# A cached-attention decode step with a gated FFN on one core: the order of the key transposes, the place of the PV matmuls, a layout of the FFN rows and a slot for the down weights

## The chip, the cores and the metric

The kernel runs on one core of a Trainium2 chip. The metric is device time in microseconds (us), the median of several executions. Five engines run their own instruction streams and meet only in semaphores: PE (TensorE, matmul), DVE (VectorE), ACT (ScalarE), POOL (GpSimd) and SP (SyncE, which here only issues DMAs).

## The reference

Four tokens (one for each of four batches) pass through two branches, which a gate mixes.

```python
q = (x @ wq)                                   # 4 x 32 heads x 128
k, v = k_cache[:, :, -4096:, :], v_cache[...]  # 8 key heads per batch, each for 4 query heads
p = softmax(q k^T / sqrt(128));  a = (p v) @ wo
gate = x @ W_gate; up = x @ W_up               # 512 -> 1792
b = (relu(gate) * up) @ W_down                 # 1792 -> 512
out = g * a + (1 - g) * b,  g = sigmoid(sum(x * gate_w))
```

All inputs are bf16. Keys and values of the window are 4 x 8 x 4096 x 128 each, so that nearly all of the 81 MB that the kernel reads is cache.

## The kernel before, in words

The 32 pairs of batch and key head are worked off in eight **sets** of four heads (s = 0 to 7; `NSET`). One set's keys are 4 MiB, and so are its values. SP issues every load, in the order of `_dma_order`: k0, x, gate_w, wq, k1, v0, then k(s), v(s-1) for s = 2 to 7, then the gate and up weights (wg, wu), v7, the down weights (wd) and the output weights (wo, in six pieces, `WO_PIECES`). The large loads go in turn into four slots of SBUF (`_slots`); a load waits until the slot's former content has been used: keys until their fourth transpose, values until the set's PV matmuls are done, wq until Q, wg until the gate and up matmuls. SP is one queue, so a load that waits holds back all that follow. In the kernel before, wd has no slot: it goes into the tile `kt`, over the transposed keys, and so waits for the last score matmul of set 7; wo takes the next slot in turn, which k7 held.

The work of the engines is written as one list of items (`_order`, L139). PE runs the items in this order, and the lists of DVE and ACT are derived from it: an item of PE appends the items of the other engines that evacuate it. For one set the items are:

- `KT(s, f)`, f = 0 to 3 (DVE, `EKT`, L506): transposes block f of the keys from the slot into `kt[:, f]`. It waits for the load of the keys and for the last reader of that part of `kt`, `SC(s-1, f)`.
- `SC(s, f)` (PE): eight matmuls of 512 columns and one for a mask, into one of three PSUM banks. DVE evacuates it (`ESC`, L534) into `sc` and keeps the row maximum. `ESC(s, 0)` waits for `EXP(s-1)`, because there is one tile `sc`.
- after `SC(s, 3)`: `MAX` (DVE, L538 and L540), `SW` (one small matmul that spreads the maxima over the rows of a head), `ESW` (DVE, L545 and L546, which gives `negmax`) and `EXP` (ACT, L612, `pe` from `sc`).
- `PT(s)` (DVE, `EPT`, L550): transposes `pe` into `pT`. There is one tile `pe`, so that `EXP(s)` waits for `PT(s-1)`.
- `RS(s)`: a small matmul for the sums of the rows; DVE makes the reciprocal.
- `PV(s)` (PE): 32 matmuls of 512 columns on the values of set s. ACT scales the result (`NORM`, L590), `OQ(s)` (16 small matmuls) turns it, ACT copies it (`EOQ`, L597).

Set s is pipelined against set s-1 by the list: in the loop over s, the softmax and PV of set s-1 stand between the score blocks of set s. The list of the kernel before is, for s from 1:

```python
o += [("KT", s, 0), ("PT", s - 1), ("KT", s, 1), ("SC", s, 0), ("KT", s, 2), ("SC", s, 1), ("KT", s, 3), ("SC", s, 2)]
o += [("RS", s - 1), ("PV", s - 1), ("SC", s, 3), ("SW", s), ("OQ", s - 1)]
```

After set 7 follow `PT(7)`, `RS(7)`, `GU` (gate and up matmuls: for each 16 matmuls, four column groups of the array side by side, the four groups taking 448 neighbouring columns each), ReLU on ACT (L605) and the product on DVE (`H`, L558), `HT` (56 matmuls of 4 columns that turn the rows of h), `PV(7)`, `OQ(7)`, `FFN` (28 matmuls with wd), `T2` (DVE, L566) and `WO` (64 matmuls, piece by piece as wo lands). `FIN` (L570) mixes, and two stores end the program. All matmuls are issued by one helper, which is why they share L314.

Of the kernel before, what the change touches and what calls it, by code (L numbers as in the profile page):

```python
# [8 lines left out]
ALU = mybir.AluOpType  # L9
# [128 lines left out]

def _order():  # L139
    o = [("XT",), ("Z",), ("KT", 0, 0), ("KT", 0, 1), ("KT", 0, 2), ("KT", 0, 3), ("Q",), ("QT",)]  # L140
    o += [("SC", 0, f) for f in range(4)] + [("SW", 0)]
    for s in range(1, NSET):
        o += [("KT", s, 0), ("PT", s - 1), ("KT", s, 1), ("SC", s, 0), ("KT", s, 2), ("SC", s, 1), ("KT", s, 3), ("SC", s, 2)]
        o += [("RS", s - 1), ("PV", s - 1), ("SC", s, 3), ("SW", s), ("OQ", s - 1)]
    s = NSET - 1
    o += [("PT", s), ("RS", s), ("GU",), ("HT",), ("PV", s), ("OQ", s), ("FFN",)]
    return o + [("WO", p) for p in range(len(WO_PIECES))]


# [7 lines left out]
def _slots():  # L157

    frees = [[] for _ in range(NSLOT)]
    at, wait = {}, {}  # L160
    turn = 0
    for it in _dma_order():
        k = it[0]
        if k in ("x", "gw", "wd") or (k == "wo" and it[1] > 0):
            continue
        if k == "wu":
            at[it] = at[("wg",)]
            wait[it] = wait[("wg",)]
# [5 lines left out]
        frees[n] = {"k": [("E", "KT", it[-1], 3)], "v": [("PV", it[-1])], "wq": [("Q", 1)], "wg": [("GU", 1)], "wo": []}[k]  # L174
    return at, wait


def _program(nc, plan, R, aps):
# [16 lines left out]

    Wq = slot("wq").rearrange("p (t f) -> p t f", t=4)
    Wg, Wu = slot("wg")[:, 0:4 * FF], slot("wg")[:, 4 * FF:8 * FF]
    Wd = kt[:, :, :].rearrange("p f c -> p (f c)")[:, 0:14 * 512]
    Wo = slot("wo", 0).rearrange("p (i c) -> p i c", i=32)
    grelu, hrow = sc[:, 0:448], sc[:, 512:960]  # L200

    trf, scf = {}, {}
    for it in order:
# [39 lines left out]
    def sync(e):  # L243
# [5 lines left out]
        for it in _dma_order():  # L249
# [4 lines left out]
            elif k == "gw":  # L254
                load(("GW",), "d_gw", gwT[:, :], gate_w.rearrange("(p t) -> p t", t=4))
            elif k == "wq":
                load(("WQ",), "d_wq", slot("wq"), A_wq.rearrange("(p t) f -> p (t f)", t=4), waits=w)
            elif k == "wg":
                load(("WG",), "d_wg", Wg, B_W_gate.rearrange("(p t) f -> p (t f)", t=4), waits=w)
            elif k == "wu":  # L260
                load(("WU",), "d_wu", Wu, B_W_up.rearrange("(p t) f -> p (t f)", t=4), waits=w)
            elif k == "wd":
                load(("WD",), "d_wd", Wd, B_W_down.rearrange("(p i) c -> p (i c)", i=14),
                     waits=[("SC", NSET - 1, 3)])
            elif k == "wo":
# [44 lines left out]
    def tensor(t):  # L310
# [73 lines left out]
        def OQ(s):  # L384
            key = ("OQ", s)
            r = 64 * (s // 4)
            for t in range(2):
                for cc in range(2):
                    for c in range(4):
# [106 lines left out]
    def vector(v):  # L496
# [58 lines left out]
            E.op(lambda: v.reciprocal(recip[:, s % 2:s % 2 + 1], banks[tr(key)][:, 0:1]), ev=("E",) + key, waits=[key])  # L555

        def H():
            E.op(lambda: v.tensor_tensor(hrow, grelu, banks[scb(("GU", 1))][:, 0:448], ALU.mult), ev=("H",),  # L558
                 waits=[("RELU",), ("GU", 1)])
            plan.ev[("E", "GU", 1)] = plan.ev[("H",)]  # L560

        def EHT():
            E.op(lambda: v.tensor_copy(hT[:, :], banks[tr(("HT",))][:, 0:56]), ev=("E", "HT"), waits=[("HT",)])
# [13 lines left out]
    def scalar(a):  # L577
# [24 lines left out]
                     ev=("GE",) if u else None, waits=[("Z",)])  # L602

        def RELU():
            E.op(lambda: a.activation(grelu, banks[scb(("GU", 0))][:, 0:448], ACTF.Relu), ev=("RELU",),  # L605
                 waits=[("GU", 0), ("EXP", NSET - 1)])
            plan.ev[("E", "GU", 0)] = plan.ev[("RELU",)]

# [41 lines left out]
```

## Time and profile before

| what | value |
|---|---|
| median of 3 runs | 207.85 us (207.54 to 209.7) |
| the profiled execution: own time, span | 209.0 us, 207.3 us |
| busy, of the span | PE 136.1 us (66%), DVE 127.0 us (61%), ACT 31.3 us (15%) |
| DMA | 81.16 MB, 392 GB/s over the span, 92.3% of 16 engines' span |
| mean granted PE clock | 0.876 |

The span is the time from the first to the last instruction of the profiled execution, and its own time is what was measured around it. A busy share is an average over the whole span: it tells that no single compute engine is full, not what each stage waits for. For that one reads the chain of waits, which goes back from the last instruction to what released it each time, and windows, which give busy time, granted clock and DMA rate of one stretch. SP's rows tell when a load was issued; the DMA view gives the time from the issue to the landing. PE's clock is granted by a throttle: 1.00 is full and 0.50 half.

### The profile page before, as it was taken

Reading aid. Unit: us, or ns where it says so; the run is one execution under the profiler, and the core shown is the slowest. Engines: PE = TensorE matmul, PEld = TensorE weight load, DVE = VectorE, ACT = ScalarE, POOL = GpSimd, SP = SyncE. Lnnn points to the kernel's source line nnn. Section 1 sums busy time; section 2 is a strip of 40 time slices with the busy share of each in tenths; the row PEclk is TensorE's granted clock in tenths of the full one; section 3 lists DMA queues with packets and bytes.
Section 4 is the critical chain, followed back from the end, with each engine's and each line's share of the span. In section 5 each row is a group of like instructions: output and inputs, shape, how many; then the busy total and the mean of one; then the engine's idle time right before and its main releaser. Section 6 shows DMA issues by size and latency. Waiting matters only on the chain.

```text
span 207.3 us, 2287 instructions
## 1 busy us (share of the span) xinstructions
PE 136.1 (66%) x936; PEld 60.8 (29%) x936; DVE 127.0 (61%) x193; ACT 31.3 (15%) x72; POOL 14.0 (7%) x38
## 2 busy tenths in 40 slices
PE   0010363991798459758966793789399766956975
PEld 0000131330243214322522251243234322522543
DVE  6039382128982997299649936991998299525000
ACT  2000036004001400140022014001400140033010
POOL 7774000000000000000000000000000000000000
PEclk9999995599589988967996999699769969996699
DMA  5999999999977999999999999999999999849950
GB/s 202 462 418 430 413 411 462 436 408 444 443 335 304 405 506 402 335 436 417 405 411 477 424 411 432 455 424 408 468 424 424 396 443 443 373 123 417 422 215 1
DMA packets 3923, 81.16 MB, mean 392 GB/s; under 512 B 572, under 2 KB 584, under 8 KB 968
## 3 DMA queue, kind: packets, MB, share of 16 engines
q1 hardware_dynamic: 3904, 81.01, 92.3%
q8 instruction: 7, 0.11, 0.2%
q14 instruction: 4, 0.03, 0.0%
q10 hardware_dynamic: 8, 0.00, 0.0%
HBM read 81.01 MB, written 0.00 MB: 391 GB/s over the span
## 4 chain that ended last, share of the span: by engine, by line
PE 46%; DVE 37%; DMA 10%; issue 3%; ACT 2%; SPq 1%; DVEq 0%; ACTq 0%
PE bank L314 45%; DVE kt L506 20%; DMA slots<-in_A_wq_dram 10%; DVE pT L550 8%; DVE sc L534 4%; DVE qblk L493 2%; ACT pe L612 1%; PE bank L318 1%; ACT qblk L587 1%; DVE rd L540 1%; SPq L247 1%; DVE hmax L545 1%; DVE negmax L546 1%; DVE rowmax L538 1%; ACT osb L590 0%
## 5 line engine op out<-in xcount | busy, mean ns | idle before, releaser
L314 PE MATMUL bank<-kt,qblk 128*128 128x512 bf16 x256 | 75.8, 446 | 27.0 <-DVE kt L506 24.9
L506 DVE STREAM_TRANSPOSE kt<-slots 128x2048 f32<-128x2048 f32 x32 | 73.2, 2294 | 0.0
L534 DVE TENSOR_SCALAR_CACHE_REDUCE sc<-bank 128x512 bf16<-128x512 f32 x32 | 21.4, 668 | 41.6 <-PE bank L314 41.6
L314 PEld LDWEIGHTS bank<-kt,qblk 128*128 128x128 bf16 x256 | 25.4, 108 | 72.5 <-DVE kt L506 33.5
L314 PE MATMUL bank<-slots,pT 128*64 128x512 bf16 x256 | 30.4, 393 | 0.0
L612 ACT ACTIVATE pe<-sc,negmax 128x2048 bf16<-128x2048 bf16 x8 | 16.0, 2002 | 35.7 <-DVE negmax L546 35.7
L590 ACT ACTIVATE osb<-bank,recip 128x512 bf16<-128x512 f32 x8 | 5.5, 687 | 101.6 <-PE bank L314 101.6
L550 DVE STREAM_TRANSPOSE pT<-pe 128x2048 bf16<-128x2048 bf16 x8 | 18.5, 2312 | 2.2 <-ACT pe L612 2.2
L314 PEld LDWEIGHTS bank<-slots,pT 128*64 128x64 bf16 x256 | 14.3, 113 | 12.4 <-issue 1.5
L314 PE MATMUL bank<-maskr,maskl 128*128 128x512 bf16 x32 | 13.6, 424 | 0.0
L314 PE MATMUL bank<-slots,xT 128*4 128x512 bf16 (+1 forms) x64 | 6.4, 571 | 9.6 <-DMA slots<-in_A_wq_dram 9.6
L318 PE MATMUL bank<-identb,xsb 4*128 4x4 bf16 x4 | 0.3, 173 | 13.4 <-DMA xsb<-in_A_x_dram 13.4
L314 PE MATMUL bank<-rd,grpb 128*128 128x8 bf16 x8 | 1.3, 168 | 10.9 <-DVE rd L540 9.3
L314 PE MATMUL bank<-osb,fold 128*64 128x32 bf16 x128 | 5.4, 184 | 0.8 <-ACT osb L590 0.8
L314 PEld LDWEIGHTS bank<-slots,xT 128*4 128x4 bf16 x64 | 1.8, 111 | 12.5 <-DMA slots<-in_A_wq_dram 9.7
L566 DVE TENSOR_SCALAR t<-bank,gg 128x256 f32<-128x256 f32 x1 | 0.5, 484 | 7.8 <-PE bank L314 7.8
L510 DVE COPY xT<-bank 128x16 bf16<-128x16 bf16 x1 | 0.2, 167 | 8.2 <-PE bank L318 8.2
L314 PEld LDWEIGHTS bank<-osb,fold 128*64 128x64 bf16 x128 | 4.6, 112 | 1.5 <-ACT osb L590 1.3
L314 PEld LDWEIGHTS bank<-rd,grpb 128*128 128x128 bf16 x8 | 0.8, 95 | 14.7 <-issue 12.9
L314 PEld LDWEIGHTS bank<-maskr,maskl 128*128 128x128 bf16 x32 | 3.4, 106 | 5.3 <-issue 2.5
L493 DVE COPY qblk<-bank 32x32 bf16<-32x32 bf16 x32 | 4.0, 179 | 0.9 <-PE bank L318 0.8
L318 PEld LDWEIGHTS bank<-identb,xsb 4*128 4x128 bf16 x4 | 0.2, 115 | 13.4 <-DMA xsb<-in_A_x_dram 13.4
(56 smaller groups left out, 63.9 us busy)
## 6 DMA issues: line engine op xcount, KB each, us to landing
slots<-in_A_k_cache_dram SPq DMA_DIRECT2D x8, 4096.0 KB, 15.9
slots<-in_A_v_cache_dram SPq DMA_DIRECT2D x8, 4096.0 KB, 22.5
slots<-in_A_wq_dram SPq DMA_DIRECT2D x1, 4096.0 KB, 21.4
slots<-in_A_wo_dram SPq DMA_DIRECT2D x3, 1024.0 KB, 12.0
slots<-in_B_W_gate_dram SPq DMA_DIRECT2D x1, 1792.0 KB, 10.7
slots<-in_B_W_up_dram SPq DMA_DIRECT2D x1, 1792.0 KB, 14.6
kt<-in_B_W_down_dram SPq DMA_DIRECT2D x1, 1792.0 KB, 7.0
slots<-in_A_wo_dram SPq DMA_DIRECT2D x1, 512.0 KB, 14.6
```

The costliest lines, as they stand in the source:

```text
L247: E.op(lambda: e.dma_start(dst, src), ev=ev, waits=waits, ctr=ctr)
L314: E.op(lambda: t.matmul(out_, lhsT, rhs, start=start, stop=stop, tile_position=pos, skip_group_check=True), ev=ev, waits=waits)
L318: E.op(lambda: t.transpose(out_, in_, idn), ev=ev, waits=waits)
L493: E.op(lambda dst=dst, r=r, g=g, e=e, src=src: copy(dst, src[r, g, 0:B, e, :, :]), ev=("E",) + key if (q, g, e) == (3, 1, 1) else None, wa ...
L506: E.op(lambda: v.transpose(kt[:, f, :].bitcast(FP32), slot("k", s)[:, 4096 * f:4096 * f + 4096].bitcast(FP32)), ev=("E", "KT", s, f), waits=w)
L534: E.op(lambda: v.tensor_scalar(sc[:, 512 * f:512 * f + 512], banks[scb(key)], 1.0, None, op0=ALU.mult, op1=ALU.max, accum_out=mx4[:, f:f + ...
L538: E.op(lambda: v.tensor_reduce(rowmax[:, :], mx4[:, :], AXIS.X, ALU.max), ev=("RMX", s), waits=[("E", "SC", s, 3)])
L540: E.op(lambda: v.tensor_scalar(rd8[:, :], R["own8"][:, :], rowmax[:, 0:1], None, op0=ALU.mult), ev=("MAX", s), waits=[("RMX", s), ("OWN", ...
L545: E.op(lambda: v.tensor_reduce(hmax[:, :], banks[tr(key)][:, 0:8], AXIS.X, ALU.max), ev=("E",) + key, waits=[key])
L550: E.op(lambda: v.transpose(pT[:, s % 2, :], pe[:, :]), ev=("E", "PT", s), waits=[("EXP", s)] + ([("PV", s - 2)] if s >= 2 else []))
L590: E.op(lambda: a.activation(osb[:, s % 2, :], ob(s), ACTF.Copy, scale=recip[:, s % 2:s % 2 + 1]), ev=("NORM", s), waits=[("E", "RS", s), ( ...
L612: E.op(lambda: a.activation(pe[:, :], sc[:, :], ACTF.Exp, bias=negmax[:, s % 2:s % 2 + 1], scale=SCALE, accum_out=rowsum[:, s % 2:s % 2 + ...
```

## The change

Four things are changed.

1. **The order of the list.** `KT(s, 0)` stands ahead of `SC(s-1, 3)`, so that on DVE the first key transpose of the next set runs before the fourth score block of the set before it is evacuated. `PV(s-1)` stands behind `SC(s, 2)` as before, but `SC(s, 3)` is now in the next turn of the loop, behind `KT(s+1, 0)`. `OQ` stands ahead of `SW`, and `PT(s-1)` behind `KT(s, 1)`.
2. **A slot for wd.** wd takes the next slot in turn, the one of k7, and so waits for the fourth key transpose of set 7; wo moves to the slot that v6 held, and waits for `PV(6)`.
3. **GU by residues.** Column group j takes the 128 columns of each index i = j, j+4, ... instead of 448 neighbouring ones. The moving operand is read with a step of 14 elements (28 bytes), in 512 columns (j = 0, 1) or 384 (j = 2, 3) instead of 448.
4. **HT whole.** Four transposes of 128 x 128 in place of 56 small matmuls; `RELU` and `H` work on 512 columns instead of 448, and the copy `EHT` picks the 56 columns from the bank.

```diff
 def _order():
-    o += [("SC", 0, f) for f in range(4)] + [("SW", 0)]
+    o += [("SC", 0, 0), ("SC", 0, 1), ("SC", 0, 2)]
     for s in range(1, NSET):
-        o += [("KT", s, 0), ("PT", s - 1), ("KT", s, 1), ("SC", s, 0), ("KT", s, 2), ("SC", s, 1), ("KT", s, 3), ("SC", s, 2)]
-        o += [("RS", s - 1), ("PV", s - 1), ("SC", s, 3), ("SW", s), ("OQ", s - 1)]
+        o += [("KT", s, 0), ("SC", s - 1, 3)] + [("OQ", s - 2)] * (s > 1) + [("SW", s - 1), ("KT", s, 1), ("PT", s - 1)]
+        o += [("SC", s, 0), ("KT", s, 2), ("SC", s, 1), ("RS", s - 1), ("KT", s, 3), ("SC", s, 2), ("PV", s - 1)]
     s = NSET - 1
-    o += [("PT", s), ("RS", s), ("GU",), ("HT",), ("PV", s), ("OQ", s), ("FFN",)]
+    o += [("SC", s, 3), ("OQ", s - 1), ("SW", s), ("PT", s), ("RS", s), ("GU",), ("HT",), ("PV", s), ("OQ", s), ("FFN",)]
...
-        if k in ("x", "gw", "wd") or (k == "wo" and it[1] > 0):
+        if k in ("x", "gw") or (k == "wo" and it[1] > 0):
...
-    Wd = kt[:, :, :].rearrange("p f c -> p (f c)")[:, 0:14 * 512]
+    Wd = slot("wd")[:, 0:14 * 512]
...
-                     waits=[("SC", NSET - 1, 3)])
+                     waits=w)
...
+        def gu_n(j):
+            return 512 if j < 2 else 384
+
+        def gu_cols(W, q, j):
+            g = W[:, FF * q:FF * q + FF].rearrange("p (k i) -> p i k", i=14)
+            return g[:, j:14:4, :]
...
-                        mm(banks[scb(fill)][32 * j:32 * j + 4, 0:448], xT[:, 4 * q:4 * q + 4],
-                           W[:, FF * q + 448 * j:FF * q + 448 * j + 448], q == 0, q == 3,
+                        mm(banks[scb(fill)][32 * j:32 * j + 4, 0:gu_n(j)], xT[:, 4 * q:4 * q + 4],
+                           gu_cols(W, q, j), q == 0, q == 3,
...
-            for i in range(14):
-                for j in range(4):
-                    r = slice(32 * j, 32 * j + 4)
-                    mm(banks[tr(key)][32 * j:32 * j + 32, 4 * i:4 * i + 4], hrow[r, i:448:14], identb[r, r], True, True,
-                       ev=key if (i, j) == (13, 3) else None, waits=tr_free(key) + [("H",), ("IDB",)],
-                       pos=(32 * j, 32 * j))
+            for g in range(4):
+                tp(bankb[tr(key)][:, 128 * g:128 * g + 128], hrow[:, 128 * g:128 * g + 128], identb[:, :],
+                   ev=key if g == 3 else None, waits=tr_free(key) + [("H",), ("IDB",)])
```

How the list moves the instructions is shown at three places. The first is DVE in the middle of the program, one turn of the loop, from the evacuation of the fourth score block of a set on; `kt<-slots` is a key transpose, `pT<-pe` the transpose of the probabilities, `sc,mx4<-bank` the evacuation of a score block, `rowmax` to `negmax` the softmax's maxima. Before:

```order
L534 TENSOR_SCALAR sc,mx4<-bank4 128x512
L538 TENSOR_REDUCE rowmax<-mx4 128x1
L540 TENSOR_SCALAR rd8<-own8,rowmax 128x8
L545 TENSOR_REDUCE hmax<-bank1 128x1
L546 TENSOR_SCALAR negmax<-hmax 128x1
L506 STREAM_TRANSPOSE kt<-slots 128x2048
L550 STREAM_TRANSPOSE pT<-pe 128x2048
L506 STREAM_TRANSPOSE kt<-slots 128x2048
L534 TENSOR_SCALAR sc,mx4<-bank2 128x512
L506 STREAM_TRANSPOSE kt<-slots 128x2048
L534 TENSOR_SCALAR sc,mx4<-bank3 128x512
L506 STREAM_TRANSPOSE kt<-slots 128x2048
```

And the same turn in the changed kernel, whose lines are four further down for the same code:

```order
L510 STREAM_TRANSPOSE kt<-slots 128x2048
L538 TENSOR_SCALAR sc,mx4<-bank4 128x512
L542 TENSOR_REDUCE rowmax<-mx4 128x1
L544 TENSOR_SCALAR rd8<-own8,rowmax 128x8
L549 TENSOR_REDUCE hmax<-bank0 128x1
L550 TENSOR_SCALAR negmax<-hmax 128x1
L510 STREAM_TRANSPOSE kt<-slots 128x2048
L554 STREAM_TRANSPOSE pT<-pe 128x2048
L538 TENSOR_SCALAR sc,mx4<-bank2 128x512
L510 STREAM_TRANSPOSE kt<-slots 128x2048
L538 TENSOR_SCALAR sc,mx4<-bank3 128x512
```

Between `negmax` and the third key transpose of the set there stood two key transposes and `pT`; now one key transpose and `pT`, and the first key transpose stands ahead of the fourth evacuation.

The second place is PE over the same stretch; `slots,pT` is PV, `kt,qblk` with `maskr,maskl` a score block, `rd8,grpb` is SW, `osb,fold` OQ and `rowsum,grpf` RS. Before:

```order
L314 MATMUL bank6<-slots,pT 64x512 x32
L314 MATMUL bank3<-kt,qblk 128x512 x8
L314 MATMUL bank3<-maskr,maskl 128x512
L314 MATMUL bank0<-rd8,grpb 128x8
L314 MATMUL bank1<-osb,fold 64x32 x16
L314 MATMUL bank4<-kt,qblk 128x512 x8
```

In the changed kernel:

```order
L314 MATMUL bank5<-slots,pT 64x512 x32
L314 MATMUL bank4<-kt,qblk 128x512 x8
L314 MATMUL bank4<-maskr,maskl 128x512
L314 MATMUL bank1<-osb,fold 64x32 x16
L314 MATMUL bank0<-rd8,grpb 128x8
L314 MATMUL bank2<-kt,qblk 128x512 x8
```

On PE, OQ now stands ahead of SW (and RS, outside these rows, one score block earlier); the first score block of the next set follows as before, but the key transpose that it waits for now stands earlier on DVE.

The third place is the end of SP's queue, with the engine that each load waits for:

```order
 L247 DMA slots<-in_A_v_cache_dram 128x1x16384 [waits pe]
-L247 DMA kt<-in_B_W_down_dram 128x7168 [waits pe]
-L247 DMA slots<-in_A_wo_dram 128x4096 [waits dve]
+L247 DMA slots<-in_B_W_down_dram 128x7168 [waits dve]
+L247 DMA slots<-in_A_wo_dram 128x4096 [waits pe]
 L247 DMA slots<-in_A_wo_dram 128x4096 x2
```

The down weights wait for DVE (the last key transpose) instead of PE (the last score block), and the first piece of wo for PE (`PV(6)`).

More of the change, by code (lines that the diff above doesn't have):

```diff
@@ L173, in _slots @@
         wait[it] = list(frees[n])
-        frees[n] = {"k": [("E", "KT", it[-1], 3)], "v": [("PV", it[-1])], "wq": [("Q", 1)], "wg": [("GU", 1)], "wo": []}[k]
+        frees[n] = {"k": [("E", "KT", it[-1], 3)], "v": [("PV", it[-1])], "wq": [("Q", 1)], "wg": [("GU", 1)], "wd": [], "wo": []}[k]
     return at, wait
@@ L197, in _program @@
     Wg, Wu = slot("wg")[:, 0:4 * FF], slot("wg")[:, 4 * FF:8 * FF]
-    Wd = kt[:, :, :].rearrange("p f c -> p (f c)")[:, 0:14 * 512]
+    Wd = slot("wd")[:, 0:14 * 512]
     Wo = slot("wo", 0).rearrange("p (i c) -> p i c", i=32)
-    grelu, hrow = sc[:, 0:448], sc[:, 512:960]
+    grelu, hrow = sc[:, 0:512], sc[:, 512:1024]
     trf, scf = {}, {}
@@ L557, in H @@
         def H():
-            E.op(lambda: v.tensor_tensor(hrow, grelu, banks[scb(("GU", 1))][:, 0:448], ALU.mult), ev=("H",),
+            E.op(lambda: v.tensor_tensor(hrow, grelu, banks[scb(("GU", 1))], ALU.mult), ev=("H",),
                  waits=[("RELU",), ("GU", 1)])
@@ L562, in EHT @@
         def EHT():
-            E.op(lambda: v.tensor_copy(hT[:, :], banks[tr(("HT",))][:, 0:56]), ev=("E", "HT"), waits=[("HT",)])
+            ht_src = bankb[tr(("HT",))][:, 0:512].rearrange("p (i x) -> p i x", x=32)[:, 0:14, 0:4]
+            E.op(lambda: v.tensor_copy(hT[:, :].rearrange("p (i b) -> p i b", b=4), ht_src), ev=("E", "HT"), waits=[("HT",)])
         def T2():
@@ L604, in RELU @@
         def RELU():
-            E.op(lambda: a.activation(grelu, banks[scb(("GU", 0))][:, 0:448], ACTF.Relu), ev=("RELU",),
+            E.op(lambda: a.activation(grelu, banks[scb(("GU", 0))], ACTF.Relu), ev=("RELU",),
                  waits=[("GU", 0), ("EXP", NSET - 1)])
```

## The prediction

> **What bounds the kernel now.** I read the stages first, because the page's busy shares (PE 66%, DVE 61%) name no engine. Each row gives a stretch, its length, the busy time of PE, its weight loads, DVE, ACT and POOL, then the granted PE clock, the DMA share and GB/s: an early stretch, the one around the third key load, four whole sets, and the last set.
>
> ```profile
> 36.00:55.00 19.00, 13.95 (x46) 4.97 (x44) 9.80 (x15) 2.09 (x2) 0.00 (x0) 0.77 1.01 436
> 55.00:68.65 13.65, 11.97 (x76) 5.46 (x77) 8.18 (x17) 0.69 (x1) 0.00 (x0) 0.87 0.85 350
> 88.78:166.05 77.27, 58.84 (x353) 25.06 (x351) 57.49 (x74) 11.73 (x16) 0.00 (x0) 0.87 1.00 428
> 166.05:185.38 19.33, 14.37 (x93) 6.27 (x91) 14.37 (x18) 3.02 (x4) 0.00 (x0) 0.91 0.86 348
> ```
>
> Over four sets the DMA engines are full at 428 GB/s; around the third key load and in the last set they lose 15% of 13.65 us (2.05 us) and 14% of 19.33 us (2.7 us). Yet the chain that ended last holds no DMA in the middle of the program, only DVE and PE. One set of it (start, length, what):
>
> ```profile
> 108.10 2.22 DVE kt L506
> 110.32 2.26 DVE pT L550
> 112.58 2.19 DVE kt L506
> 114.77 0.59 DVE sc L534 x2
> 115.36 2.23 DVE kt L506
> 117.59 0.05 issue
> 117.64 7.89 PE bank L314 x52
> ...
> 125.56 0.71 DVE sc L534 x2
> ...
> 127.42 2.22 DVE kt L506
> ```
>
> A set takes 127.42 - 108.10 = 19.32 us: three key transposes and `pT` in a row, then score block 2, RS, PV and score block 3 on PE (7.89), then the softmax's small steps (1.86 from 125.56). A set moves two loads of 4.194 MB, at 428 GB/s 19.6 us. So two loops of almost the same length run side by side, and each hides the other. The start and the end of the chain, after which the stores remain:
>
> ```profile
> 48.71 2.22 DVE kt L506
> ...
> 68.65 2.22 DVE kt L506
> ...
> 185.40 2.10 ACT pe L612 x2
> ...
> 187.64 3.08 PE bank L314 x34
> ...
> 190.82 0.63 DVE sc L558
> ...
> 191.59 5.90 PE bank L314 x88
> ...
> 197.57 0.70 ACT osb L590
> ...
> 198.31 2.30 PE bank L314 x44
> ...
> 201.24 3.68 PE bank L314 x64
> ...
> 204.94 0.48 DVE osum L570
> ```
>
> 3.08 is RS and GU, 5.90 HT and PV(7), 2.30 OQ and FFN, 3.68 WO. Then SP's rows (issue times) and the DMA view's times from issue to landing, for v1, v7, wd and the last two pieces of wo, in this order:
>
> ```profile
> 27.54 0.54 SPq L247 DMA_DIRECT2D slots<-in_A_v_cache_dram  x1
> 62.11 0.53 SPq L247 DMA_DIRECT2D slots<-in_A_k_cache_dram  x1
> 162.12 0.54 SPq L247 DMA_DIRECT2D slots<-in_A_v_cache_dram  x1
> 183.50 0.33 SPq L247 DMA_DIRECT2D kt<-in_B_W_down_dram  x1
> ```
>
> ```profile
> L247 SPq DMA_DIRECT2D slots<-in_A_wo_dram x6: 432/456/674, 183.9 to 186.6; - x6
> ```
>
> ```profile
> slots<-in_A_v_cache_dram SPq DMA_DIRECT2D x1, 4096.0 KB, 36.2
> ...
> slots<-in_A_v_cache_dram SPq DMA_DIRECT2D x1, 4096.0 KB, 21.6
> ...
> kt<-in_B_W_down_dram SPq DMA_DIRECT2D x1, 1792.0 KB, 7.0
> ...
> slots<-in_A_wo_dram SPq DMA_DIRECT2D x2, 256.0 KB, 14.8
> ```
>
> v1 lands at 27.54 + 36.2 = 63.7, k3 was issued only 1.6 us ahead of that, and the queue ran dry: the first loss. v7 lands at 183.7, while wd was issued at 183.50, behind score block 3 of set 7: the second loss. The last piece of wo lands at 186.6 + 14.8 = 201.4, just when the WO matmuls begin (201.24).
>
> **The change part by part.** *The loop of the engines.* The first key transpose leaves the chain: it now runs under PE's 7.89 us, where DVE has besides it two evacuations (2 x 0.59), one key transpose (2.2) and a reciprocal (0.1): 5.7 us in all. `EXP` (2.10) hides under the key transpose that now stands between `negmax` and `pT` (2.2). The loop becomes 19.32 - 2.22 = 17.10 us. No instruction is added. The moved transpose has a wait of its own, the landing of the next keys, and behind it on DVE are queued the fourth evacuation and the whole softmax, for which ACT and PV wait. So it may start 2.2 us late before it delays anything, and without that cover it costs its 2.22 again.
>
> *The start.* In set 0 the moved transpose delays the fourth evacuation, which nothing covers there:
>
> ```profile
> 44.63 0.69 DVE L534 TENSOR_SCALAR_CACHE_REDUCE sc<-bank 128x512 bf16<-128x512 f32 x1 [1.25 <-PE bank L314]
> ...
> 46.59 0.69 DVE L534 TENSOR_SCALAR_CACHE_REDUCE sc<-bank 128x512 bf16<-128x512 f32 x1 [1.25 <-PE bank L314]
> ```
>
> It ends at 44.63 + 0.69 + 2.22 = 47.54 instead of 46.59 as the evacuation's start, so set 0's softmax is 0.95 late: 49.66. Set 1 took 68.65 - 48.71 = 19.94, now 17.72: its softmax ends at 67.4, 1.3 ahead. The fourth transpose, whose end releases k3, is done 2.22 + 2.26 + 0.59 + 2.23 + 0.59 + 2.23 = 10.1 after set 0's maxima, at 59.8, where k3 was issued at 62.11.
>
> *The load queue.* What follows v1 is 12 transfers of 4.194 MB and three weights of 1.835, 55.8 MB. At 428 GB/s without a hole that is 130.5 us: the last piece would land at 63.7 + 130.5 = 194.2. From the other side: from 201.4 I take off only what the two losses show, 2.5 for wd (it landed 6.8 us after v7, its bytes need 4.3) and 1.6 of the 2.05 of the first: 197.3. I take 195.5, nearer to the rate of four sets than to the sum of the holes, since a rest of the first hole stays (k3 is issued near 60, when the first of the 16 engines are already through with v1). wd now waits for the last key transpose and wo for `PV(6)`, both long done when v7 lands (below); SP holds nothing else behind them.
>
> *Do the engines keep up?* By themselves they would have set 7's maxima at 67.4 + 6 x 17.10 = 170.0 (185.38 before). But k7 is the ninth transfer after v1, 88.2 us, and lands at about 63.7 + 88.2 + 1.3 = 153.2 with the same rest of a hole; set 7's first transpose may start without harm until 67.4 + 4 x 17.10 + 12.97 = 148.8 (12.97 = 2.22 + 2.26 + 0.59 + 2.23 + 7.89 - 2.22, the way from set 5's maxima to 2.22 ahead of the end of the 7.89). It waits 4.4: maxima at 174.4, `EXP` done 176.5. This is the wait that takes the old one's place, and it costs nothing as long as the loads set the end.
>
> *GU and HT.* GU streams the same number of columns in groups of 512 instead of 448: 3.08 x 512/448 = 3.5, done at 180.1. No moving operand here has a step of 28 bytes. The nearest rows are weight loads, one of 32 columns in steps of 28 bytes, one of 64 neighbouring columns, and the GU matmuls themselves:
>
> ```profile
> L314 PEld LDWEIGHTS bank<-osb,fold 128*64 128x64 bf16 x32 | 1.2, 112 | 1.4 <-ACT osb L590 1.3
> ...
> L314 PEld LDWEIGHTS bank<-identb,sc 4*32 4x32 bf16 x56 | 0.9, 149 | 1.7 <-issue 1.7
> ```
>
> If I put the excess of the strided load over the other, 37 ns, on its 32 columns, it is 1.2 ns a column on top of the 0.86 that one costs in GU now (3.08 us over eight groups of 448): 2.0 x 512 x 8 = 8.3 us. From below it is the 3.08 as they are. I keep 3.5: in the 7.89 us, 18 score matmuls, whose moving operand takes every second element, and 32 of PV, two side by side, make 34 streams of 512 columns of 0.23 us each, so a step by itself costs nothing there. The 8.3 goes into the range. HT and PV(7) share 5.90, and this row is PV's part:
>
> ```profile
> 192.52 4.94 PE L314 MATMUL bank<-slots,pT 128*64 128x512 bf16 x32
> ```
>
> So HT's 56 small matmuls took 1.0 us; the four transposes, without a row of their own, lie between nothing and that, and I take 0.8. `H` grows by a seventh of its 0.63. With these PV(7) could start at 181.8; both edits together move it by less than 0.3.
>
> [...]
>
> *The end.* v7 lands at 63.7 + 49.8 MB / 428 + 1.3 = 181.4, as late as PV(7) is ready for it. From 181.8 on: PV 4.9, `NORM` and its wait 0.8, OQ and FFN 2.3, `T2` 0.6, so WO may begin at 190.4 and all its matmuls would be done at 194.1, ahead of the last landing at 195.5 by 1.4. So only the last piece remains: 4 of 64 matmuls 0.2, `osum` 0.5, the stores 207.3 - 205.4 = 1.9, hops 0.1, in all 2.7 where 5.9 stood (207.3 - 201.4).
>
> **The sum.** Last landing 201.4 to 195.5: 5.9. The WO queue behind it: 3.2. Together 9.1 off the span of 207.3, so 198.2. The profiled execution's own time was 209.0 and becomes 199.9; the median of the runs, 207.85, becomes 198.75. I predict 198.7 us.
>
> **The rivals.** *A: PE's clock.* These rows cut the trace at the instants at which the clock changes, every 3.41 us:
>
> ```profile
> 72.28:75.69 3.41, 1.09 (x6) 0.35 (x5) 3.41 (x3) 0.00 (x0) 0.00 (x0) 1.00 1.07 461
> 75.69:79.11 3.42, 3.42 (x10) 1.17 (x9) 2.44 (x3) 0.00 (x0) 0.00 (x0) 0.50 1.06 460
> ...
> 123.48:126.89 3.41, 2.07 (x10) 0.75 (x10) 1.08 (x4) 0.69 (x1) 0.00 (x0) 1.00 1.00 432
> ```
>
> After a window with 1.09 us of matmuls the clock halves for the next one, after one with 2.07 it doesn't. In the new loop PE has a hole of about 2.8 us, between score block 1 (done 4.4 after the maxima) and block 2 (7.3 after them), and the half-clock window then falls on blocks 2, PV and 3, all on the chain: 3.41/2 = 1.7 us for a hit. Half of the six sets hit would be 5.1 us and stay inside the 4.4 that set 7 waits and the 1.4 at the end. If all six are hit, the maxima come at 170.0 + 10.2 = 180.2, past 175.8 by 4.4: 203.1 us. For it speaks that the hole is longer than the 2.3 us of idle time in the first of these rows; against it, that a hole which two windows share leaves both of them busier, and that the windows shift from set to set. [...]
>
> *B: GU at 8.3 us.* PV(7) starts 4.8 later, 1.4 of it hidden: 198.7 + 3.4 = 202.1.
>
> *C: slower.* The clock stays at half for two windows in a row over the 7.89 of every set: 3.4 us a set, 67.4 + 6 x 20.5 = 190.4 for the maxima, and the old 21.9 behind them: about 213 us. It decides from (185.38 - 67.4)/6 - 17.10 = 2.6 us lost a set. Against it: the window after 75.69 is full of matmuls and the clock is back right behind it.
>
> *D: no change.* The moved transpose waits for its keys in every set, the loop becomes the load loop of 19.6, the maxima come at 67.4 + 6 x 19.6 = 185.0 and the tail behind them is as before: 207.5. Against it: k3 lands near 63.7 + 1.3 + 9.8 = 74.8, and set 3's transpose isn't due before 67.4 + 12.97 = 80.4.
>
> **How the numbers follow.** Forecast 0.66, A 0.17, B 0.08, C 0.04, D 0.05. A change of 1%, 2.1 us, is about what a measurement of this kernel tells from none. Forecast, A and B are faster by more: 0.91; D is the same, 0.05; C is slower, 0.04. The likeliest case's own range is 195.0 (the early stretch's 436 GB/s for all that follows v1 and no rest of the first hole: 63.7 + 128.1 + 2.7, plus the 0.5 between span and median) to 200.5 (the landing at 197.3). Out to A and B it becomes 195.0 to 204.0.
>
> **What would show it.** Right: no stretch under 0.95 of DMA share between v1 and the last piece but a short one near 62; chain steps of 17.1 to 18.8 us in sets 2 to 5, and DVE or PE waiting for a key load from set 6 on; wd issued near 167 instead of 183.50; the last WO matmuls waiting for a piece of wo. Wrong: no engine ever waits for a load after set 1, and WO's 64 matmuls still run as one block (A or B, told apart by the granted clock in the 7.89 and by GU's duration); or DMA share below 0.95 in the middle sets (C).

## The result and the profile after

| what | before | after |
|---|---|---|
| median, same chip | 208.73 us (4 runs, 207.54 to 209.7) | 200.49 us (4 runs, 198.78 to 200.92) |
| ratio, 95% interval | | 0.9593 [0.9507, 0.9678] |
| the profiled execution: own time, span | 209.0 us, 207.3 us | 200.62 us, 198.8 us |
| DMA over the span | 392 GB/s, 92.3% | 408 GB/s, 95.6% |
| mean granted PE clock | 0.876 | 0.948 |

The forecast was 198.7 us in a range of 195.0 to 204.0, faster with 0.91. In the kernels called slot, GU, half values and fill below, half or more of the executions lie over 1.5% above the fastest, so that their ratios rest on few executions; there the median of all and the profiled execution are read.

First the stages, in the columns of the prediction's windows. The cuts are the ends of the sets' maxima, so that rows 2 to 6 are one set each (sets 2, 3, 5, 6 and 7).

```profile
55.00:65.55 10.55, 8.80 (x69) 4.20 (x71) 8.01 (x15) 0.92 (x2) 0.00 (x0) 1.00 1.00 401
65.55:82.47 16.92, 12.40 (x87) 5.84 (x87) 14.38 (x19) 3.01 (x4) 0.00 (x0) 1.00 1.00 431
82.47:99.40 16.93, 12.62 (x88) 5.83 (x87) 14.47 (x20) 3.02 (x4) 0.00 (x0) 1.00 1.00 433
...
116.75:135.90 19.15, 12.35 (x87) 5.68 (x87) 14.12 (x18) 3.02 (x4) 0.00 (x0) 1.00 1.01 432
135.90:155.60 19.70, 14.41 (x89) 6.46 (x89) 14.62 (x21) 3.02 (x4) 0.00 (x0) 0.91 1.00 428
155.60:174.16 18.56, 13.86 (x85) 5.90 (x83) 12.27 (x17) 3.02 (x4) 0.00 (x0) 0.91 1.01 429
```

Both DMA holes are gone: the share is 1.00 around the third key load (0.85 before) and all the way to set 7. The sets begin at the pace of the engines, 16.9 us, and in sets 5 and 6 go at that of the loads, 19.2 to 19.7. Set 7 has its keys and still takes 18.56, at a mean clock of 0.91. Then the chain that ended last: one set of it, the two key loads in it, and the end.

```profile
65.55 2.22 DVE kt L510
67.77 2.25 DVE pT L554
70.02 0.59 DVE sc L538 x2
70.61 2.22 DVE kt L510
...
82.47 2.22 DVE kt L510
...
92.67 20.07 DMA slots<-in_A_k_cache_dram
...
126.95 24.64 DMA slots<-in_A_k_cache_dram
151.61 2.31 DVE kt L510
...
192.78 3.68 PE bank L314 x64
```

Between the maxima and the evacuation at 70.02 there stood two key transposes and `pT`; now one and `pT`. Two key loads now stand in the chain, the second, of set 7's keys, from its issue at 126.95 to its landing at 151.59, where DVE's next transpose had waited for it; before, no load stood in the middle of the program. The end, though, is not a load: the 64 WO matmuls run as one block of 3.68 us. The reason is on PE: score block 2 of set 7, GU and PV(7) in the timeline (start, length, number of matmuls, and in brackets the idle time ahead and what ended it):

```profile
162.95 3.20 PE L314 MATMUL bank<-kt,qblk 128*128 128x512 bf16 x8 [2.83 <-DVE kt L510]
...
176.65 7.51 PE L314 MATMUL bank<-slots,xT 128*4 128x512 bf16 x32
...
185.36 3.64 PE L314 MATMUL bank<-slots,pT 128*64 128x512 bf16 x32
```

GU takes 7.51 us where 3.5 was forecast. And in set 7 the clock halved over score block 2 (0.50 from 163.37 to 166.78), which takes 3.20 us instead of 1.91; this makes the set 18.56 long instead of 16.93. Then the queue of the loads: SP's rows of the down weights and the six pieces of wo, then the time from issue to landing of the last pieces.

```profile
165.79 0.33 SPq L247 DMA_DIRECT2D slots<-in_B_W_down_dram  x1
170.31 2.70 SPq L247 DMA_DIRECT2D slots<-in_A_wo_dram  x6
```

```profile
slots<-in_A_wo_dram SPq DMA_DIRECT2D x2, 256.0 KB, 22.1
```

The last piece is issued near 172.6 (the sixth of six in 170.31 to 173.0) and lands 22.1 later, at 194.7, 6.7 us earlier than the 201.4 of before. Its four WO matmuls (0.40 us in the next run) could have been through near 195.2. They are through at 196.46, since the block began only at 192.78.

### The profile page after: what moved, and what is told of

The parts are those of the page before. It is cut to its first block, busy times and chain, and to the rows that moved or that the text cites. A ratio compares the mean times of both kernels' runs of the same rounds, so it can differ in the third digit from the quotient of the medians.

```text
span 198.8 us, 2166 instructions
## 1 busy us (share of the span) xinstructions
PE 126.6 (64%) x875; PEld 57.3 (29%) x884; DVE 127.0 (64%) x193; ACT 31.8 (16%) x72; POOL 14.0 (7%) x38
## 3 DMA queue, kind: packets, MB, share of 16 engines
q1 hardware_dynamic: 3904, 81.01, 95.6%
## 4 chain that ended last, share of the span: by engine, by line
DVE 35%; DMA 33%; PE 18%; another core or an unknown queue 6%; issue 3%; ACT 2%; SPq 1%; DVEq 0%; ACTq 0%
DMA slots<-in_A_k_cache_dram 22%; DVE kt L510 18%; PE bank L314 17%; DMA slots<-in_A_wq_dram 11%; DVE pT L554 7%; DVE sc L538 5%; DVE qblk L497 2%; PE bank L318 1%; ACT pe L617 1%; ACT qblk L592 1%; SPq L247 1%; DVE rd L544 1%; DVE hmax L549 1%; DVE negmax L550 0%
## 5 line engine op out<-in xcount | busy, mean ns | idle before, releaser
L314 PE MATMUL bank<-kt,qblk 128*128 128x512 bf16 x256 | 66.2, 402 | 25.6 <-DVE kt L510 23.3
L314 PEld LDWEIGHTS bank<-kt,qblk 128*128 128x128 bf16 x256 | 23.5, 100 | 59.8 <-DVE kt L510 27.8
L314 PE MATMUL bank<-slots,pT 128*64 128x512 bf16 x256 | 29.3, 382 | 0.1
L314 PEld LDWEIGHTS bank<-slots,pT 128*64 128x64 bf16 x256 | 13.8, 110 | 15.1 <-issue 3.6
L314 PE MATMUL bank<-slots,xT 128*4 128x512 bf16 (+1 forms) x64 | 10.8, 784 | 9.7 <-DMA slots<-in_A_wq_dram 9.7
L314 PE MATMUL bank<-maskr,maskl 128*128 128x512 bf16 x23 | 9.2, 399 | 0.0
L562 DVE TENSOR_TENSOR sc<-sc,bank 128x512 bf16<-128x512 bf16 x1 | 0.7, 687 | 5.6 <-remote 5.6
```

The costliest lines, as they stand in the source:

```text
L314: E.op(lambda: t.matmul(out_, lhsT, rhs, start=start, stop=stop, tile_position=pos, skip_group_check=True), ev=ev, waits=waits)
```

## The experiments

Two theories on what sets the end stand against each other. **L**: in the changed kernel the load queue sets it, and the order of the list has won the time by keeping the queue full. **E**: the engines' loop still sets it, and the time is won because the loop is shorter. A third question is GU's price. The runs are told in the order in which they ran; kernels of one group share their runs of the kernel before (207.47 us for the first four, 206.91 for the next four, 208.15 for the last).

**Order alone** (the kernel before and the change's first part, nothing else).

```diff
-        o += [("KT", s, 0), ("PT", s - 1), ("KT", s, 1), ("SC", s, 0), ...
-        o += [("RS", s - 1), ("PV", s - 1), ("SC", s, 3), ("SW", s), ("OQ", s - 1)]
+        o += [("KT", s, 0), ("SC", s - 1, 3)] + [("OQ", s - 2)] * (s > 1) + [("SW", s - 1), ("KT", s, 1), ("PT", s - 1)]
+        o += [("SC", s, 0), ("KT", s, 2), ("SC", s, 1), ("RS", s - 1), ("KT", s, 3), ("SC", s, 2), ("PV", s - 1)]
```

> The order of the list alone: wd still goes into kt behind the last score block of set 7, GU and HT are as before. Theory L (the loads set the end once the engines' loop is shorter, and GU by residues costs 4.4 us at the end, 7.51 against 3.08): score block 3 of set 7 is done near 172, ahead of v7's landing at 180.5, so wd is in the queue in time without a slot; last landing 194.7, behind it 2.7, span 197.4, some 1.4 us under the changed kernel's 198.8. Rival S (the slot closes the last hole): a hole of 2.5 us stays in the queue, span 199.9 or more. Rival E (the engines' chain sets the end): 198.8 - 4.4 + 0.6 = 195.0.

Measured: 198.54 us (198.15 to 199.39), ratio 0.9557 [0.9507, 0.9608]. The order by itself brings all of the gain. Its span of 196.4 lies 1.0 below L's figure and 1.4 above E's, so that the chain has to decide. Its wd still goes over the transposed keys and waits for the last score block, but that is done earlier; SP's row and the end of its chain:

```profile
171.96 0.33 SPq L247 DMA_DIRECT2D kt<-in_B_W_down_dram  x1
```

```profile
174.71 18.88 DMA slots<-in_A_wo_dram
...
193.63 0.40 PE bank L314 x4
```

wd is issued at 171.96, more than 11 us sooner than before (183.50). And here the end is what was forecast for the changed kernel: four WO matmuls wait for the last piece, 0.40 us, and only `osum` and the stores follow.

**Slot alone** (the kernel before and the second part).

```diff
-    Wd = kt[:, :, :].rearrange("p f c -> p (f c)")[:, 0:14 * 512]
+    Wd = slot("wd")[:, 0:14 * 512]
...
-                     waits=[("SC", NSET - 1, 3)])
+                     waits=w)
```

> The slot for wd alone, in the old order. Theory L: wd is issued near 178.3 (last key transpose) instead of 183.5 and lands before 189, but FFN waits for PV(7) and OQ at 198.3 anyway, so the span stays at 207.3 within 0.5 and WO runs as one block. Rival S: the load queue ends 2.5 us earlier and so does the kernel, span 204.8.

Measured: median 208.03 us of ten (204.09 to 209.65) beside 207.47; the ratio 0.9892 [0.9821, 0.9963] rests on the two lowest, the other eight lie between 207.56 and 209.65. wd is issued at 177.56 instead of 183.50, and the end stays what it was:

```profile
200.43 3.68 PE bank L314 x64
```

An earlier wd is worth nothing here, because WO waits for the engines: the whole block of 64 follows FFN.

**GU and HT alone** (the kernel before and the third and fourth part).

```diff
-                        mm(banks[scb(fill)][32 * j:32 * j + 4, 0:448], ...
-                           W[:, FF * q + 448 * j:FF * q + 448 * j + 448], q == 0, q == 3,
+                        mm(banks[scb(fill)][32 * j:32 * j + 4, 0:gu_n(j)], ...
+                           gu_cols(W, q, j), q == 0, q == 3,
```

> GU by residues and HT whole alone, in the old order. Theory L: GU lies on the chain of the kernel before, takes about 7.5 us instead of 2.8 to 3.1, HT gains 0.6, PV(7) behind it perhaps 1.3 because the clock is up by then: span 207.3 + 4.4 - 0.6 - 1.3 = 209.8, from 209.5 to 211.5. Rival (the long GU of the changed kernel came from the loads that land at the same time, not from the step of 28 bytes): GU stays near 3.5, span 206.7 to 207.3.

Measured: median 212.18 us (208.96 to 213.28) beside 207.47, profiled span 210.5 beside 205.8. By itself this part makes the kernel slower, by about 4.7 us. In the profiles 2.9 of that lie behind set 7's maxima (from there to the first WO matmul 18.8 us instead of 15.9); where the rest comes from is not shown. GU has the same length as in the changed kernel, where other loads run beside it:

```profile
188.23 7.50 PE L314 MATMUL bank<-slots,xT 128*4 128x512 bf16 x32
```

**Changed without GU and HT** (order and slot).

```diff
-                        mm(banks[scb(fill)][32 * j:32 * j + 4, 0:gu_n(j)], ...
-                           gu_cols(W, q, j), q == 0, q == 3,
+                        mm(banks[scb(fill)][32 * j:32 * j + 4, 0:448], ...
+                           W[:, FF * q + 448 * j:FF * q + 448 * j + 448], q == 0, q == 3,
```

> The changed kernel with GU and HT as before (order and slot stay). Theory L: GU ends near 179.7 instead of 184.2, PV(7) starts near 181.4, at v7's landing; the last WO matmuls wait for the last piece of wo, which lands at 194.7, and the span is 197.4. Rival E (the loads don't set the end): the whole 4.4 less 0.6 comes off, span 195.0. Rival W (the long GU keeps the clock up and so pays for itself): span 198.5 or more.

Measured: 198.36 us (198.07 to 198.97), ratio 0.9547 [0.9499, 0.9595], the same as the order alone: the slot brings nothing on top of it either. In this execution PE's clock halved over the critical matmuls of three sets (granted 0.51 from 90.3 to 97.1 and 0.50 from 110.7 to 114.1, in the second and third of them). Two of the pieces in its chain, a set without and a set with the half clock:

```profile
74.20 7.77 PE bank L314 x50
...
110.90 9.33 PE bank L314 x50
...
171.24 22.61 DMA slots<-in_A_wo_dram
```

Three such sets cost 1.6, 2.9 and 1.6 us in the loop (9.40, 10.62 and 9.33 against 7.77), and yet the span is 196.7 (L had 197.4, E 195.0) and the last piece of wo ends it. The waits for keys shrink instead: 1.8 us in one wait, 12.0 in three in the changed kernel. This is what L says.

**1.2 us more on DVE in each set** (the one before, with half of `pT` transposed twice).

```diff
+            E.op(lambda: v.transpose(pT[:, s % 2, 0:1024], pe[:, 0:1024]), ev=("XPT", s), ...
             E.op(lambda: v.transpose(pT[:, s % 2, :], pe[:, :]), ev=("E", "PT", s),
```

> The kernel of the run without the GU edit (order and slot changed, GU and HT as before, span 196.7), and in each set the first half of pT is transposed once more, ahead of the whole one: about 1.2 us more on DVE in each set's chain. Theory L (the loads pace the kernel; the engines' loop of 16.9 has 2.5 us of play against the loads' 19.4): the loop becomes 18.1, the waits for keys shrink, the span stays at 196.7 to 198. Theory E (the engines' chain sets the end): seven times 1.2, span 205.

Measured: 214.34 us (213.63 to 216.49), ratio 1.0394 [1.0304, 1.0485]. Neither theory has this: 16 us more than without it (span 211.9), of which the added instructions, if nothing hid them, are 7 x 1.2 = 8.4. Two neighbouring clock windows, then score block 2 on PE, then five sets in one row:

```profile
73.55:76.96 3.41, 0.39 (x2) 0.21 (x3) 3.41 (x5) 0.00 (x0) 0.00 (x0) 1.00 1.05 452
76.96:80.37 3.41, 3.41 (x10) 1.04 (x10) 2.49 (x5) 0.00 (x0) 0.00 (x0) 0.50 0.96 413
...
87.77:189.80 102.03, 73.74 (x429) 31.25 (x432) 76.47 (x95) 15.09 (x20) 0.00 (x0) 0.85 0.97 406
```

```profile
76.57 3.27 PE L314 MATMUL bank<-kt,qblk 128*128 128x512 bf16 x8 [4.11 <-DVE kt L506]
```

PE's hole ahead of score block 2 grew to 4.11 us, the window that lies in it holds 0.39 us of matmuls, and the next window runs score block 2 and PV at half clock. That happened in every set, and a set takes 102.03/5 = 20.4 us: 16.93, 1.2 for the instruction and about 2.3 for the clock. The loads' 19.6 no longer cover it, and the DMA share falls to 0.97.

**2.3 us more on DVE in each set** (all of `pT` twice).

```diff
+            E.op(lambda: v.transpose(pT[:, s % 2, 0:2048], pe[:, 0:2048]), ev=("XPT", s), ...
             E.op(lambda: v.transpose(pT[:, s % 2, :], pe[:, :]), ev=("E", "PT", s),
```

> As the run with 1.2 us more, but all of pT is transposed twice: about 2.3 us more in each set. Theory L: the loop becomes 19.2 to 19.3, no more than the loads' 19.4 from set to set, but all of it lies ahead of the set 7 that waited before: maxima of set 7 at 65.5 + 2.3 + 6 x 19.25 = 183.3 instead of 174, engine-bound tail of 21 to 22 us behind, span 204 to 206. So the first 1.2 us cost nothing and the second 7 to 9. Theory E: both doses cost the same, 8 each, span 213.

Measured: 222.09 us (221.97 to 222.55), ratio 1.0756 [1.0691, 1.0822], with a mean clock of 0.876 and steps of 20.6 to 22.2 us in the chain. Its span of 220.3 lies 7 us above E's figure and 14 to 16 above L's, and its score blocks 2 are slow as well: in the chain each takes with the mask 3.42 to 4.04 us from 79.19 on (3.10 to 4.04 in the run before). The next 1.1 us a set cost 7.75 us, about the instructions themselves (7 x 1.1 = 7.7); the large jump belongs to the first 1.2.

**Half of the values** of sets 2 to 6 (order and slot; PV reads former contents in the other half, so its output isn't the reference's).

```diff
+                half = k == "v" and 2 <= it[1] < NSET - 1
+                dst, rows = (slot(*it)[:, 0:8192], src[0:4, :, :]) if half else (slot(*it), src)
```

> The kernel without the GU edit, and of the values of sets 2 to 6 only the first half is loaded (PV reads old content in the rest): 10.5 MB less, 24 us of the load queue. Theory L: no engine waits for keys any more, the engines' loop sets the end: maxima of set 7 at 65.5 + 6 x 16.92 = 167.1 or some clock hits of 1.7 later, then EXP, GU, HT, PV, OQ, FFN and WO one behind the other, 21.5: span 188.6 to 192. Theory E (the loads were hidden): the span stays at 196.7.

Measured: median 195.75 us of four (192.09 to 198.16), the profiled one 193.76 with a span of 192.1, at the upper end of L's range. With less to load the end comes earlier, so the loads did set it. What sets it now is the loop of the engines; five sets in one window:

```profile
85.59:170.27 84.68, 62.73 (x429) 28.94 (x431) 69.70 (x89) 15.09 (x20) 0.00 (x0) 1.00 0.90 374
```

84.68/5 = 16.94 us a set, and the DMA share is 0.90. So the play between the loops is about 19.6 - 16.9 = 2.7 us a set.

**`pT` ahead of the second key transpose** (order and slot, one pair turned round).

```diff
-... + [("SW", s - 1), ("KT", s, 1), ("PT", s - 1)]
+... + [("SW", s - 1), ("PT", s - 1), ("KT", s, 1)]
```

> The kernel without the GU edit, with one item moved back: the transpose of the probabilities stands ahead of the second key transpose again, so nothing on DVE covers EXP. Theory L: the 2.1 us of EXP enter the chain in place of the key transpose that left it, the loop is 19.0 to 19.1, maxima of set 7 at 65.5 + 2.1 + 6 x 19.05 = 181.9, span 203 to 205: the first key transpose's move alone gains nothing in the loop. Rival (the key transpose's move is what counts): span 196.7 to 198.

Measured: 215.96 us (215.39 to 218.62), ratio 1.0434 [1.0333, 1.0534]: slower than the kernel before, and with a span of 214.6, 10 to 12 us beyond L's figure. The chain of a set, and five sets in one window:

```profile
68.90 2.10 ACT pe L612 x2
71.03 2.31 DVE pT L550
...
89.43 2.10 ACT pe L612 x2
```

```profile
89.40:191.80 102.40, 72.41 (x429) 31.97 (x431) 70.36 (x89) 15.09 (x20) 0.00 (x0) 0.83 0.97 405
```

`EXP` is in the loop again, as expected, which makes it 19.0. The other 1.5 us of the 20.5 go with a clock of 0.83. So moving the key transpose is only half of what the order does; that a second one covers `EXP` is the other half.

**What a step in the moving operand costs** (order and slot; the eight groups of GU read their 448 columns in steps of 1, 2, 4, 7, then 8, 14, 28 and 1 elements, other columns than the reference's).

```diff
-                           W[:, FF * q + 448 * j:FF * q + 448 * j + 448], ...
+            for n, (W, key, steps) in enumerate(((Wg, "WG", (1, 2, 4, 7)), (Wu, "WU", (8, 14, 28, 1)))):
+                        o, c = args(W, fill, q, j, steps[q])
```

> The kernel without the GU edit; the eight groups of GU (four matmuls side by side, 448 columns each) read their moving operand in steps of 1, 2, 4, 7 elements (gate) and 8, 14, 28, 1 (up), other columns than the reference's, so that the FFN branch is not the reference's. Theory P (a fixed price for each 16-byte line that a step touches): steps 1, 2 and 4 take what the full or half clock gives (0.19 or 0.37 us a group), 8, 14 and 28 all take 0.92, the mean of the changed kernel (7.51 us over eight groups), 7 slightly less. Rival F (any step above 2 costs the same): 4 takes 0.92 as well. Rival G (the price grows with the step): 28 takes twice what 14 does.

Measured, in one execution of 199.51 us, with the clock at 0.50 over all of these matmuls:

```profile
176.23 0.54 PE L421 MATMUL bank<-slots,xT 128*4 128x448 bf16 x4
176.56 0.59 PE L423 MATMUL bank<-slots,xT 128*4 128x448 bf16 x4
176.94 0.58 PE L425 MATMUL bank<-slots,xT 128*4 128x448 bf16 x4
177.33 0.88 PE L427 MATMUL bank<-slots,xT 128*4 128x448 bf16 x4
178.03 0.98 PE L429 MATMUL bank<-slots,xT 128*4 128x448 bf16 x4
178.81 0.99 PE L431 MATMUL bank<-slots,xT 128*4 128x448 bf16 x4
179.62 0.96 PE L433 MATMUL bank<-slots,xT 128*4 128x448 bf16 x4
180.38 0.56 PE L435 MATMUL bank<-slots,xT 128*4 128x448 bf16 x4
```

The rows overlap, so read from start to start: 0.33 us with neighbouring columns, 0.38 and 0.39 with steps of 4 and 8 bytes, 0.70 with 14, then 0.78, 0.81 and 0.76 with 16, 28 and 56. The price nearly doubles between 8 and 14 bytes and is flat from 16 on. That fits theory P, a price for each new stretch of 16 bytes: with 14 bytes seven of eight columns touch a new one, and 7/8 of the 0.78 to 0.81 is 0.68 to 0.71. It doesn't fit a price that grows with the step. What in the hardware makes the price, and what steps of 4 and 8 bytes cost at full clock, this run doesn't show.

**Fill the hole** (the kernel with 1.2 us more, and eight matmuls without use, into the bank that FFN later starts anew, behind `RS` in sets 0 to 6).

```diff
+            for _ in range(8 if s < NSET - 1 else 0):
+                mm(banks[ACC], R["maskl"][:, :], R["maskr"][:, :], True, True, ...
```

> The run with 1.2 us more on DVE in each set (span 211.9), and eight idle matmuls (into the bank of the FFN, before it is used) behind RS, in the hole in which PE waits for the third key transpose; DVE has the same work. Theory K (the 1.2 us cost so much because they widened PE's hole from 2.8 to 4.1 us, after which the clock halved over score block 2 and PV in every set): the hole is 2.4, the clock stays at 1.00 between 60 and 170, the loop is 18.1, the span 196.7 to 199.5. Rival (the longer chain on DVE itself costs it): 211 to 212, whatever the clock.

Measured: median 206.63 us of ten (203.52 to 208.71), where 214.34 stood without the fill. That is half of the loss, not all of it: five of seven sets were still hit (9.40 and 9.41 us in the chain, against 7.78 in the other two). But one execution now has both kinds, one set after the other:

```profile
88.35:106.56 18.21, 14.53 (x97) 6.46 (x96) 15.63 (x21) 3.02 (x4) 0.00 (x0) 1.00 0.99 418
106.56:126.41 19.85, 16.16 (x97) 6.80 (x96) 15.75 (x21) 3.02 (x4) 0.00 (x0) 0.91 1.01 436
```

At full clock (1.00) the set takes 18.21, which is 16.93 + 1.2; when hit (a mean of 0.91) it takes 1.6 more. So the clock is the cause of what neither theory had (the other 1.2 is the instruction itself), while the fill is a poor remedy: a hole of 2.36 us was left ahead of score block 2.

**The changed kernel and order with slot once more, on one chip.** No edit against the changed kernel in the one; in the other GU and HT are as before.

```diff
-                           gu_cols(W, q, j), q == 0, q == 3,
+                           W[:, FF * q + 448 * j:FF * q + 448 * j + 448], q == 0, q == 3,
```

> The changed kernel once more, beside the kernel without the GU edit on the same chip. Both theories: span 198.8, ratio to the kernel before 0.955 to 0.963.

> The kernel without the GU edit (order and slot) once more, as the candidate that beats both. Theory L: 1.5 to 2.4 us under the changed kernel on the same chip, since only 2 of GU's 4.4 us stick out behind the loads; ratio to the kernel before 0.948 to 0.956. Rival E (the engines' chain sets the end): 3.8 us under it.

Measured: 199.76 us (199.07 to 200.99), ratio 0.9617 [0.9568, 0.9666], and 198.33 us (198.09 to 199.0), ratio 0.9537 [0.9494, 0.958]. Six executions each, and the two ranges don't meet, if only by 0.07 us: GU's layout and HT together cost 1.4 us in the changed kernel, just under what L had. The WO matmuls at the end of the two profiles, first with GU's layout, then without:

```profile
191.30 3.68 PE bank L314 x64
```

```profile
194.51 0.40 PE bank L314 x4
```

Of these two, the second has the slower PV(7) (5.54 us, against 3.64 in the first) and the lower mean clock (0.922, against 0.939). Still the one without the layout ends on the last piece, and the one with it on the block of 64, which waited for no piece. So GU's length by itself is enough to put the end on the engines. The best version is the order without the rest; the order alone (198.54) and with the slot (198.36, 198.33) can't be told apart.

## Why the prediction was right, and where it was off

**The mechanism.** The time moved from the engines' loop to the load queue, as forecast. Shown by three runs: the order alone gives it, fewer bytes make the kernel faster still, and three hits of the clock inside one execution change the waits for keys but not the end. In the changed kernel itself the queue sets the time up to the landing of set 7's keys, and the engines' tail with the long GU sets the last 1.4 us. The higher mean clock (0.948 after 0.876) is not what shortened the loop: in the sets of the kernel before, the half clock fell on the first score blocks (block 0 took 3.31 us at 110.38, with 0.50 from 109.83 to 113.24), which its chain doesn't contain, and the 7.89 us that the chain does contain are at full clock (1.00 from 117.64 to 125.53). Only in the tail did it lie in the chain, over PV(7) (0.60 from 192.5 to 195.9), with 4.94 us instead of 3.64.

**The sum.** Forecast 5.9 for the last landing and 3.2 for what stands behind it, together 9.1. Measured 201.4 - 194.7 = 6.7 and 5.9 - (198.8 - 194.7) = 1.8, together 8.5. So the first term was 0.8 too small and the second 1.4 too large; that the sum came so near is partly luck, since the two errors lean against each other.

**The step that was mis-sized: GU.** "I keep 3.5" was wrong; it takes 7.51, near the upper end of 8.3. The rows I leaned on, matmuls that take every second element, have a step of 4 bytes, and the steps experiment shows that this is below the jump: at half clock steps of 4 and 8 bytes cost 0.05 and 0.06 us a group over the 0.33 of neighbouring columns, one of 16 bytes 0.45. So GU was nearly as long as in rival B. It cost less than B's 3.4 on the total, for PV(7) behind it ran at full clock (1.00 from 185.36 to 189.00): 3.64 instead of the 4.9 that I took from before. With GU at 3.5 and PV(7) at 4.9, WO could have begun near 190; the last piece would have ended the kernel at 194.7 + 2.7 = 197.4, 1.4 below the span of 198.8. The pair of runs on one chip measures 1.4 between the medians.

**The last WO matmuls wait for a piece** failed for the same reason: they do so in the order alone and without GU's layout, not in the changed kernel, in either of its profiles.

**The slot.** I credited 2.5 us of the landing to wd's new wait. The order does that too, by finishing the last score block at 172: order with and without slot are level, and the slot alone brings nothing.

**The loop and the waits.** Forecast 17.10, measured 16.92. The 0.95 us by which set 0 was to be late did not come (its maxima at 48.61, before at 48.71), set 1's maxima came at 65.55 instead of 67.4, so the engines ran into the loads earlier than I had it: waits at the keys of sets 5, 6 and 7, 12.0 us in all, not 4.4 at set 7 alone.

```profile
DVE kt L510 <- DMA slots<-in_A_k_cache_dram: 12.0, 3, 4.7
```

Set 7's maxima were to come at 174.4 and came at 174.16, and that is luck: the keys of set 7 landed at 151.59 instead of 153.2, and the half clock then made the set 1.6 longer. wd was issued at 165.79 (forecast 167), and the last piece landed at 194.7 (195.5).

**Rival A** came in part: not in sets 2 to 5 of the changed kernel, but in set 7. In set 2 the hole was there; score block 2 with the idle time ahead of it, and the two clock windows that share that time:

```profile
72.89 1.91 PE L314 MATMUL bank<-kt,qblk 128*128 128x512 bf16 x8 [2.82 <-DVE kt L510]
```

```profile
67.89:71.30 3.41, 2.17 (x11) 1.08 (x11) 3.41 (x4) 0.00 (x0) 0.00 (x0) 1.00 1.00 432
71.30:74.71 3.41, 1.82 (x9) 0.78 (x9) 3.41 (x5) 0.00 (x0) 0.00 (x0) 1.00 1.00 432
```

Both windows kept 1.8 to 2.2 us of work, and the clock stayed at 1.00. A set of 16.93 us is nearly five windows of 3.41 (17.1), so that once the boundary lies in the hole it stays there for some sets; this is worked out from the rows and no run sets the phase. The waits for keys then moved the sets against the windows. In set 7 the same hole lay in one window (159.96 to 163.37, with 0.58 us of matmuls), and the next one was at half clock: the 3.20 us of score block 2 above. The prediction let such hits be hidden by set 7's wait for its keys and by 1.4 us at the end; this one came after the wait, and the long GU had used up the 1.4. Without GU's layout the same loop was hit in three sets. **Rival C**, slower than before, is real, only not here: I took play in time, 2.6 us a set, for play, but 1.2 us in the wrong place (and `pT` one place earlier) was enough to have the clock halved in every set (means of 0.85 and 0.83 over five sets). The half clock followed a window with 0.39 us of matmuls there, and in the kernel before one with 1.09.

**Rival D** is half there: the moved transpose does wait for keys, but only once the engines have run ahead, and behind full DMA.

## What to carry to other kernels

When two loops of nearly equal length run side by side, ask which of them the change shortens and what the other then allows: here 2.2 us a set off the engines became 8.5 us in all, because it filled two holes in the load queue and, but for the long GU, took the engines out of the tail. Before adding or moving work on the engine ahead of critical matmuls, look at the idle hole that it leaves on PE against the clock's window of 3.41 us: 1.2 us more there cost 16. And price a strided operand by a row that has the same step, not by a row that merely has one: at half clock 448 columns cost 0.39 us with a step of 8 bytes and 0.70 with one of 14.

## What the runs showed of the hardware that was not expected

- Four matmuls side by side with steps of 16 bytes or more cost 0.76 to 0.81 us for 448 columns, 1.7 to 1.8 ns a column, at half clock, and 7.51/8 = 0.94 us for the longest groups of 512, 1.8 ns a column, in the changed kernel. There the clock didn't matter: the first half of GU ran mostly at 0.50, the second at 1.00, and the groups of 512 followed each other 0.93 us apart in the first and 0.91 in the second (windows of PE: length, busy time, number, clock, DMA share, GB/s).

```profile
176.65:180.48 3.83, 3.83 (x23) 0.55 0.95 401
180.48:184.20 3.72, 3.68 (x16) 1.00 0.96 400
```

- Behind the slow, strided stream PV(7) ran at full clock, 3.64 us instead of 4.9: the half clock ended at 180.5, inside GU, while in the kernel before it lay over PV(7). Whether the throttle counts the stream as work no run shows.
- After a hole of 2.36 us, with useless matmuls ahead of it, five of seven sets were still hit, while one of 2.82 us, split by a window's boundary, passed. So the length of a hole alone does not decide. Nor does the busy time of a window, as the profile counts it: of the windows at full clock, those with 1.09 and, below, with 1.73 us were followed by half clock, and the ones with 1.82 and, below, with 1.35 were not (the 1.35 stands right ahead of the prediction's window from 72.28, at 1.00). All three rows are of the kernel before; what it is that the throttle counts no run here shows.

```profile
68.87:72.28 3.41, 1.35 (x7) 0.63 (x8) 3.41 (x2) 2.03 (x3) 0.00 (x0) 1.00 1.07 461
...
85.93:89.35 3.42, 1.73 (x22) 0.89 (x20) 1.97 (x7) 0.53 (x1) 0.00 (x0) 1.00 0.97 393
89.35:92.76 3.41, 1.70 (x5) 0.58 (x6) 3.41 (x2) 1.69 (x3) 0.00 (x0) 0.50 0.96 413
```
